# Weight conversion beside the first feed-forward block: a fixed order of instructions in place of a generator, and earlier maxima in attention

## Chip, cores, metric

One core of one Trainium2 chip. The metric is the device time of one execution in microseconds; several executions of a kernel are timed and their median is given.

## What is computed

Attention over 32 heads (4 batches of 8 heads, 576 positions, 64 channels; block mask of 64 positions), then two feed-forward stages on the 2304 x 512 result:

```python
scores = where(block_i >= block_j, q @ k.T / 8, -1e9)
x = softmax(scores) @ v                                # 2304 x 512
h = x @ w_in;  x = (h * cos(h)) @ w_out                # 512 -> 2048 -> 512
P = exp(x @ w_gate - max), 8 times normalised over rows and columns
out = sum over 8 experts e of P[:, e] * (relu(x @ w1[e]) @ w2[e])
```

`w_in` and `w_out` arrive as 64-bit floats and are turned into 32-bit floats on the core ("conversion"). Each 32-bit operand of a large product is split into a high and a low part, and three products (high x high, high x low, low x high) are added in PSUM.

## The kernel before

The order on each engine is written by hand: an engine executes its instructions in the order in which the code issues them.

**Attention.** A loop runs over 32 heads. For each, PE forms trial scores (`px`, L290), DVE takes their maxima (L312) into `nm`, PE transposes them (`turn`, L317, tile `pt`), DVE writes them into the query tile (`maxima`, L321), PE computes scores (L329, then L330, which reads that query tile), ACT takes exponentials and PE multiplies with V in five pieces (`pv`, L357). Head i+1's maxima are prepared during head i: `turn` stands between pieces 3 and 4 of `pv`.

**Conversion.** The weights of the first feed-forward stage come in 32 halves of 128 x 512 numbers, each a load of 512 KB (L91). Converting one half takes two ACT instructions (L103, L109), three on DVE (L114, L118, L125) and one on POOL (L131). A generator yields these as five steps; `some` and `convert` take a number of steps from it. Eight halves are converted during attention (one in four heads), the other 24 in the first block of the feed-forward stage, two a unit. Two tiles hold loads, one tile the magnitudes (`sc`).

**First feed-forward stage.** `moe1` runs 48 units: 3 blocks of 768 tokens, in each 16 units of 128 hidden features. Unit n computes on PE the products a and b of `hidden` (two tiles `h` of 384 columns, 12 matmuls each) and then, for unit n-1, `o_part` (24 matmuls, L760, into six accumulators `acc`). Between them each product passes `reduce_h` (DVE L725 to an integer `ki`, L727 to `r`), `sine` (ACT L732), `times` (DVE L736 to `g`), `g_hi` (ACT L740 to `hh`) and `g_lo` (DVE L744 to `hl`). `wsplit` splits a converted half for PE: `jh` on ACT (L66), `jl` on POOL (L69). The weights of unit 0's hidden product are split at the end of attention into a free corner of `xh` and `xl` (`spare`).

**Queues.** SP issues all DMAs in order. An issue waits at the queue's head until the tile that it writes is free.

The rest (two more blocks, then the experts, from about 645 us on) is not changed.

Of the kernel before, what the change touches and what calls it, by code (L numbers as in the profile page):

```python
# [22 lines left out]
NC = DM // 128  # L23
# [20 lines left out]
def attention_moe_kernel(ctx: ExitStack, tc: tile.TileContext, qk, v, w_a, gate, w_b, out):  # L44
# [26 lines left out]
    raw = [None] * F1  # L71
    spare = [x[:, NC - 1, (B - 1) * S:(B - 1) * S + DM] for x in (xh, xl)]

# [4 lines left out]
    class Conv:  # L78
        def __init__(self, w64, sc):
            self.w64, self.sc, self.own = {}, {}, (w64, sc)  # L80

        def scratch(self, i, k, shape):
            n = int(np.prod(shape[1:]))
            flat = self.own[i][:, k % 2 * n:(k % 2 + 1) * n]
            return flat if len(shape) == 2 else flat.rearrange("p (n w) -> p n w", w=shape[2])

        def load(self, i):
            k = ORDER[i]
            self.w64[i] = self.scratch(0, i, [128, DM, 2])
            src = w_a[k // 2].bitcast(I32).rearrange("p (n w) -> p n w", w=2)  # L90
            nc.sync.dma_start(out=self.w64[i], in_=src[:, (k % 2) * DM:(k % 2 + 1) * DM, :])  # L91

# [6 lines left out]

        def magnitude(self, k):  # L100

            self.sc[k] = self.own[1]
            nc.scalar.activation(self.sc[k].bitcast(F32), self.high(k).bitcast(F32), AF.Abs)  # L103

        def rounding(self, k):
# [3 lines left out]
            nc.scalar.activation(w64[:, :, 0], mid, AF.Copy, scale=2.0 ** -13)  # L109

# [17 lines left out]
        def add(self, k):  # L128

            m = self.part(k).bitcast(I32)  # L130
            nc.gpsimd.tensor_tensor(out=m, in0=m, in1=self.w64.pop(k)[:, :, 0], op=ALU.add)  # L131

# [19 lines left out]
    def attention():  # L152
        with tc.tile_pool(name="at1", bufs=1) as p1, tc.tile_pool(name="at2", bufs=2) as p2, \
# [290 lines left out]
            for i in range(NH):  # L444
# [62 lines left out]
            n = F1 + 1  # L507
            return conv, conv_gen, {0: lambda: spread(e - 2), n: lambda: (x_hi(e - 4), x_lo(e - 4)), n + 1: lambda: scale(e - 2),
                              n + 2: lambda: (x_hi(e - 2), fetch(e)),
                              n + 3: lambda: (x_lo(e - 2), invert(e), give(e)), n + 4: lambda: spread(e),  # L510
                              n + 6: lambda: scale(e), n + 7: lambda: x_hi(e), n + 8: lambda: x_lo(e)}

    with tc.manual_schedule():
        conv, conv_gen, leftover = attention()
        psh = ctx.enter_context(tc.tile_pool(name="psh", bufs=2, space=PSUM))

# [4 lines left out]

        def hidden(wh, wl, t0):
            ps = psh.tile([128, TB], F32, tag="h", name="h")
# [181 lines left out]
        def moe1():  # L705
            nonlocal th, tl
            with tc.tile_pool(name="m1", bufs=2) as p:
# [6 lines left out]

                def wsplit(n, part, lo_eng=nc.gpsimd):
                    if 0 <= n < NU:
                        hi = p.tile([128, DM], F32R, tag=f"jh{part}", name="jh")
                        lo = p.tile([128, DM], F32R, tag=f"jl{part}", name="jl")
                        split(hi, lo, raw[units[n][1]][:, part * DM:(part + 1) * DM], nc.scalar, lo_eng)
                        wj[n, part] = (hi, lo)  # L720

                def reduce_h(ps):
                    ki = p.tile([128, TB], I32, tag="ki", name="ki", bufs=1)
                    r = p.tile([128, TB], F32, tag="r", name="r")
                    nc.vector.tensor_scalar(out=ki, in0=ps, scalar1=float(1 / TWO_PI), scalar2=0.25,  # L725
                                            op0=ALU.mult, op1=ALU.add)
# [47 lines left out]

                wj[0, 0] = spare
                last = NU - F1

                todo = iter(range(NH // 4 + 1, NHALF))

                def convert(n):  # L780
                    for _ in range(n):
                        next(conv_gen, None)
                    k = next(todo, None)
                    if k is not None:
                        conv.load(k)

# [12 lines left out]
                tgen = None  # L799
                convert(1)  # L800
                for n in range(NU + 1):
                    if n == F1 + 10:
                        th = post.tile([128, 3, 2, TB], F32R, tag="th", name="th", bufs=1)
                        tl = post.tile([128, 3, 2, TB], F32R, tag="tl", name="tl", bufs=1)
                        tgen = tprep(0, nc.vector)
                    if n < NU:
                        t0 = units[n][0] * HB
                        w = wj.pop((n, 0))
                        G[n] = (p.tile([128, HB], F32R, tag="hh", name="hh"),
                                p.tile([128, HB], F32R, tag="hl", name="hl"))  # L810
# [7 lines left out]
                        sine(ra)  # L818
                        if n:
                            wsplit(n + 1, 0)  # L820
                        ga = times(pa, ra)
# [239 lines left out]
```

## Time and profile before

| | us |
|---|---|
| median of 3 executions | 2176.4 (2174.54 to 2180.85) |
| the profiled execution, its time | 2170.81 |
| its span | 2169.0 |
| attention, up to the first `hidden` | 0 to 198.95 |
| first block, units 0 to 12 | 198.95 to 337.46 |
| first block, units 13 to 15 | 337.46 to 362.60 |

Busy shares of the span: PE 98%, DVE 68%, ACT 45%, POOL 41%. A row of the timeline gives start, duration, engine, source line, operation, output and inputs by the program's names, and in brackets how long the engine had been idle and what ended it. Where several like instructions follow each other they stand in one row (x2). PE's matmuls overlap; their distance from start to start says more than their durations.

### The profile page before, as it was taken

To read this page: it belongs to the slowest core of one execution; us is meant where nothing else is said; L and a number is where in the kernel's file an instruction comes from. 1 tells how busy PE (TensorE), PEld (TensorE's weight loads), DVE (VectorE), ACT (ScalarE), POOL (GpSimd) and SP (SyncE) were. 2 spreads that over 40 slices of the span, in tenths; PEclk is the share of its full clock that TensorE was granted. 3 is DMA by queue.
4 is the path that set the end of the run, shared out by engine and by line. 5 is a ranking of instruction groups with operands and counts; after the bars stand their busy time and mean duration, and the time that the engine had idled before them with its cause. 6 is when DMAs were issued, how large, how long until landed. Compare 5 with 4: busy or idle time off the path is not lost.

```text
span 2169.0 us, 29774 instructions
## 1 busy us (share of the span) xinstructions
PE 2130.2 (98%) x10959; PEld 1894.2 (87%) x10959; DVE 1474.4 (68%) x2426; ACT 968.4 (45%) x1814; POOL 899.9 (41%) x815
## 2 busy tenths in 40 slices
PE   9999889999999999999999999999999999999999
PEld 7787779998998888888898888889898888889898
DVE  7776666566667866666766666666767666666665
ACT  7886554434444333433434333433434333433432
POOL 4453443333323434434563434434563434434341
PEclk9999999999999999999999999999999999999999
DMA  6674330001001212212122211212122212212120
GB/s 166 173 182 120 101 98 1 7 1 40 1 21 59 73 64 66 71 59 78 59 78 88 74 62 63 74 59 78 59 79 88 72 65 64 73 59 78 59 78 29
DMA packets 74161, 152.84 MB, mean 70 GB/s; under 512 B 32896, under 2 KB 32896, under 8 KB 74016
## 3 DMA queue, kind: packets, MB, share of 16 engines
q1 hardware_dynamic: 74016, 150.95, 22.4%
q8 instruction: 86, 1.41, 0.3%
q14 instruction: 59, 0.48, 0.1%
HBM read 136.91 MB, written 4.87 MB: 65 GB/s over the span
## 4 chain that ended last, share of the span: by engine, by line
PE 81%; DVE 6%; issue 5%; POOL 3%; DMA 2%; ACT 2%; SPq 0%; POOLq 0%; ACTq 0%; DVEq 0%
PE acc L518 12%; PE acc L520 12%; PE acc L519 12%; PE hx L520 6%; PE hx L518 6%; PE hx L519 6%; PE acc L760 4%; PE o L357 3%; PE hy L520 3%; PE hy L518 3%; PE hy L519 3%; POOL jl L69 2%; DMA cw<-in_w_a_dram 2%; PE hz L518 1%; PE hz L520 1%
## 5 line engine op out<-in xcount | busy, mean ns | idle before, releaser
L628 POOL TENSOR_TENSOR wv<-stg,wv 128x512 fp32r<-128x512 f32 x190 | 333.7, 1778 | 853.5 <-ACT wv L627 853.5
L518 PE MATMUL acc<-wv,hh 128*128 128x512 f32 x1152 | 456.7, 396 | 0.0
L520 PE MATMUL acc<-wv,hl 128*128 128x512 f32 x1152 | 455.5, 395 | 0.0
L519 PE MATMUL acc<-wv,hh 128*128 128x512 f32 x1152 | 454.5, 395 | 0.0
L945 DVE SCALAR_TENSOR_TENSOR oa<-acc,P,oa 128x512 f32<-128x512 f32 x540 | 379.1, 740 | 4.9 <-PE acc L520 4.3
L916 ACT ACTIVATE hh<-c 128x384 fp32r<-128x384 f32 x288 | 151.3, 525 | 407.5 <-DVE c L1001 167.2
L917 DVE SCALAR_TENSOR_TENSOR hl<-c,hh 128x384 fp32r<-128x384 f32 x288 | 164.0, 569 | 176.4 <-ACT hh L916 176.4
L520 PEld LDWEIGHTS acc<-wv,hl 128*128 128x128 f32 x1152 | 216.0, 187 | 53.7
L519 PEld LDWEIGHTS acc<-wv,hh 128*128 128x128 f32 x1152 | 215.9, 187 | 43.9
L518 PEld LDWEIGHTS acc<-wv,hh 128*128 128x128 f32 x1152 | 216.1, 188 | 42.9
L69 POOL TENSOR_TENSOR jl<-raw,jh 128x512 fp32r<-128x512 f32 x95 | 131.8, 1393 | 220.1 <-ACT jh L66 214.7
L994 DVE TENSOR_TENSOR c<-hz,c 128x384 f32<-128x384 f32 x96 | 53.4, 557 | 190.8 <-PE hz L520 190.8
L619 DVE TENSOR_TENSOR wal<-s,wah 128x1024 fp32r<-128x1024 f32 x96 | 171.4, 1786 | 0.0
L984 ACT ACTIVATE c<-hx 128x384 f32<-128x384 f32 x95 | 46.9, 494 | 275.0 <-PE hx L520 275.0
L520 PE MATMUL hy<-xh,wal 128*128 128x384 f32 x384 | 128.8, 335 | 1.0 <-DVE wal L619 1.0
L518 PE MATMUL hx<-th,wah 128*128 128x384 f32 x384 | 128.7, 335 | 0.7 <-ACT c L984 0.7
L518 PE MATMUL h<-xh,jh 128*128 128x384 f32 x376 | 126.7, 337 | 2.4 <-DVE g L736 2.4
L518 PE MATMUL hy<-xh,wah 128*128 128x384 f32 x384 | 128.6, 335 | 0.4 <-DVE c L1001 0.2
L520 PE MATMUL hx<-th,wal 128*128 128x384 f32 x384 | 128.5, 335 | 0.0
L519 PE MATMUL hy<-xl,wah 128*128 128x384 f32 x384 | 128.3, 334 | 0.0
L519 PE MATMUL hx<-tl,wah 128*128 128x384 f32 x384 | 128.3, 334 | 0.0
L520 PE MATMUL h<-xh,jl 128*128 128x384 f32 x376 | 126.5, 337 | 1.6 <-POOL jl L69 1.6
(223 smaller groups left out, 4779.7 us busy)
## 6 DMA issues: line engine op xcount, KB each, us to landing
stg<-in_w_b_dram SPq DMA_DIRECT2D x192, 512.0 KB
cw<-in_w_a_dram SPq DMA_DIRECT2D x32, 512.0 KB
st<-in_qk_dram SPq DMA_DIRECT2D x64, 144.0 KB
v<-in_v_dram SPq DMA_DIRECT2D x31, 160.0 KB
tt<-inv SPq DMA_DIRECT2D x32, 144.0 KB
out_dram<-oa SPq DMA_DIRECT2D x18, 256.0 KB
kb<-qb SPq DMA_DIRECT2D x31, 144.0 KB
qb<-qa SPq DMA_DIRECT2D x31, 144.0 KB
```

The source lines that it names most:

```text
L69: eng_lo.tensor_tensor(out=lo, in0=src, in1=hi.bitcast(F32), op=ALU.subtract)
L357: nc.tensor.matmul(o[:, q0:q1], vt[:, c], e, start=c == 0, stop=True, skip_group_check=c > 0)
L518: nc.tensor.matmul(ps, lh, rh, start=first, stop=False, skip_group_check=go_on)
L519: nc.tensor.matmul(ps, lh, rl, start=False, stop=False, skip_group_check=go_on)
L520: nc.tensor.matmul(ps, ll, rh, start=False, stop=last, skip_group_check=go_on)
L619: eng.tensor_tensor(out=self.al, in0=self.s, in1=self.ah.bitcast(F32), op=ALU.subtract)
L628: eng.tensor_tensor(out=t[:, DM:2 * DM], in0=src, in1=t[:, 0:DM].bitcast(F32), op=ALU.subtract)
L760: nc.tensor.matmul(acc[half, b][:, at:at + w_], w[:, s], h[:, t0:t0 + w_], start=f == 0 and i == 0 and at == 0, stop=f == F1 - 1 and i == ...
L916: nc.scalar.activation(hh, src, AF.Relu)
L917: nc.vector.scalar_tensor_tensor(out=hl, in0=src, scalar=0.0, in1=hh.bitcast(F32), op0=ALU.max, op1=ALU.subtract)
L945: nc.vector.scalar_tensor_tensor(out=o, in0=acc, scalar=p, in1=o, op0=ALU.mult, op1=ALU.add)
L994: nc.vector.tensor_tensor(out=c[0], in0=z, in1=c[0], op=ALU.add)
```

## The change

In attention the transposition and `maxima` of the next head stand ahead of piece 3 of `pv` instead of behind it. Loads of words to convert are cut in quarters of 128 KB, one in each head from head 4 on. The last three heads split three halves into corners of `xh` and `xl` (for unit 0, both, and unit 1's hidden weights).

In the first block a function `unit` takes the place of generator and `wsplit`. 14 units convert 2, 2, 2, 1, 2, 2, 1, 2, 2, 2, 1, 2, 2, 1 halves. There are three tiles for loads (the third is `w3`) and two pairs for magnitudes and rounding words; a half's load is issued three halves ahead, and its POOL addition is made in the following unit. The first step of `reduce_h` goes from DVE to ACT, `jl` of the next hidden weights from POOL to DVE. Unit 1 puts its two products into the banks of the accumulators a11 and a12.

```diff
                 pv(i, 1)
                 pv(i, 2)
-                pv(i, 3)
                 if nxt:
                     turn(i + 1)
                     maxima(i + 1)
+                pv(i, 3)
                 pv(i, 4)
...
-                if i % 4 == 0 and i:
-                    conv.load(i // 4 + 1)
+                if i >= 4:
+                    conv.load(i // 4 + 1, None, i % 4)
...
-                if i == NH - 1:
-                    split(*spare, raw[0][:, 0:DM], nc.scalar, nc.gpsimd)
+                if i >= NH - 3:
+                    j = i - (NH - 3)
+                    f, o = FIRST[j][0], FIRST[j][1] * DM
+                    split(*SPARE[j], raw[f][:, o:o + DM], nc.scalar, nc.gpsimd)
...
+                    if by_act:
+                        nc.scalar.activation(ki, ps, AF.Identity, bias=quarter, scale=float(1 / TWO_PI))
...
+                def fetch(k):
+                    if k < NHALF:
+                        j = (k - FIRST_HALF) % 3
+                        conv.load(k, w3 if j == 2 else conv.own[0][:, j * 2 * DM:(j + 1) * 2 * DM])
+
+                def unit(n):
+                    t0 = units[n][0] * HB
+                    w = wj.pop((n, 0))
+                    ks = [todo.pop(0) for _ in range(share[n])] if n < FRAMES else []
+                    own = [pbank.tile([128, 512], F32, tag=t, name="h")[:, 0:TB] if n == 1 else None
+                           for t in ("a11", "a12")]
+                    pa = hidden(*w, t0, own[0])
+                    ra = reduce_h(pa, True)
+                    if (n, 1) not in wj:
+                        w_hi(n, 1)
+                        w_lo(n, 1)
+                    for k in adds:
+                        conv.add(k)
+                    adds[:] = ks
+                    sine(ra)
+                    pb = hidden(*w, t0 + TB, own[1])
+                    new = (n + 1, 0) not in wj
+                    if new:
+                        w_hi(n + 1, 0)
+                    ga = times(pa, ra)
+                    if new:
+                        w_lo(n + 1, 0, nc.vector)
+                    rb = reduce_h(pb, True)
+                    g_hi(n, 0, ga)
+                    g_lo(n, 0, ga)
+                    sine(rb)
+                    for k in ks[0:1]:
+                        conv.magnitude(k, more[k % 2][0])
+                    gb = times(pb, rb)
+                    g_hi(n, 1, gb)
+                    g_lo(n, 1, gb)
+                    for k in ks[1:2]:
+                        conv.magnitude(k, more[k % 2][0])
+                    for k in ks:
+                        conv.rounding(k, more[k % 2][1])
+                    for k in ks:
+                        conv.clamp(k)
+                        conv.shift(k)
+                        conv.bits(k)
+                        fetch(k + 3)
...
-                        if n == 0:
-                            wsplit(1, 0)
-                        elif units[n - 1][1]:
+                    if n < F1:
+                        unit(n)
+                    elif n < NU:
...
-                        convert(5)
                         gb = times(pb, rb)
                         g_hi(n, 1, gb)
                         g_lo(n, 1, gb)
                         if units[n][1] == 0:
                             wsplit(n, 1)
-                        convert(5)
```

On DVE a unit of the first block stood like this before (`ki`, `r`, `g` and `hl` are the steps named above, `tla` and `raw` the conversion):

```order
L725 TENSOR_SCALAR ki<-h 128x384
L727 SCALAR_TENSOR_TENSOR r<-ki,h 128x384
L736 TENSOR_TENSOR g<-h,r 128x384
L725 TENSOR_SCALAR ki<-h 128x384
L727 SCALAR_TENSOR_TENSOR r<-ki,h 128x384
L744 TENSOR_TENSOR hl<-g,hh 128x384
L114 TENSOR_SCALAR tla<-tla 128x512
L118 TENSOR_SCALAR tla<-tla 128x512
L125 SCALAR_TENSOR_TENSOR raw<-cw,tla 128x512
L736 TENSOR_TENSOR g<-h,r 128x384
L744 TENSOR_TENSOR hl<-g,hh 128x384
```

and now, in a unit with two halves (`tt` is the second magnitude tile):

```order
L744 SCALAR_TENSOR_TENSOR r<-ki,h 128x384
L753 TENSOR_TENSOR g<-h,r 128x384
L728 TENSOR_TENSOR jl<-raw,jh 128x512
L744 SCALAR_TENSOR_TENSOR r<-ki,h 128x384
L761 TENSOR_TENSOR hl<-g,hh 128x384
L753 TENSOR_TENSOR g<-h,r 128x384
L761 TENSOR_TENSOR hl<-g,hh 128x384
L114 TENSOR_SCALAR tla<-tla 128x512
L118 TENSOR_SCALAR tla<-tla 128x512
L125 SCALAR_TENSOR_TENSOR raw<-cw,tla 128x512
L114 TENSOR_SCALAR tt<-tt 128x512
L118 TENSOR_SCALAR tt<-tt 128x512
```

The `ki` rows are gone, `jl` has come, and both conversions stand behind the second `hl` instead of one between the halves of the unit and one at its end.

On ACT a unit stood like this (`jh` is the high part of the weights, `tla<-cw` the magnitude, which reads the load):

```order
L66 ACTIVATE jh<-raw 128x512
L732 ACTIVATE r<-r,half_pi 128x384
L66 ACTIVATE jh<-raw 128x512
L740 ACTIVATE hh<-g 128x384
L732 ACTIVATE r<-r,half_pi 128x384
L109 ACTIVATE cw<-cw 128x512
L103 ACTIVATE tla<-cw 128x512
L740 ACTIVATE hh<-g 128x384
L109 ACTIVATE cw<-cw 128x512
L103 ACTIVATE tla<-cw 128x512
```

and now:

```order
L740 ACTIVATE ki<-h,quarter 128x384
L723 ACTIVATE jh<-raw 128x512
L749 ACTIVATE r<-r,half_pi 128x384
L723 ACTIVATE jh<-raw 128x512
L740 ACTIVATE ki<-h,quarter 128x384
L757 ACTIVATE hh<-g 128x384
L749 ACTIVATE r<-r,half_pi 128x384
L102 ACTIVATE tla<-cw 128x512
L757 ACTIVATE hh<-g 128x384
L102 ACTIVATE tt<-w_2383 128x512
L109 ACTIVATE rawl<-cw 128x512
L109 ACTIVATE tla<-w_2383 128x512
```

The magnitude that stood last in a unit, right ahead of the next unit's `jh`, now stands ahead of the second `hh` or behind it, and the unit ends with the two roundings. `w_2383` is the third load tile.

On PE in attention the transposition `pt` stood behind the `ep` piece (128x192 or 65x192, piece 3):

```order
L290 MATMUL px<-ka,qa_99 128x320
L357 MATMUL o<-er,v_108 65x128
L357 MATMUL o<-er,v_108 65x320
L357 MATMUL o<-ec,v_108 65x320
L357 MATMUL o<-ep,v_108 65x192
L317 MATMUL pt<-ident,nm_106 101x128
L357 MATMUL o<-eq,v_108 65x64
```

and now stands ahead of it:

```order
L291 MATMUL px<-ka,qa_100 128x320
L358 MATMUL o<-er,v_109 65x128
L358 MATMUL o<-er,v_109 65x320
L358 MATMUL o<-ec,v_109 65x320
L318 MATMUL pt<-ident,nm_107 101x128
L358 MATMUL o<-ep,v_109 65x192
L358 MATMUL o<-eq,v_109 65x64
```

Only the transposition has moved, by one piece; the maxima on DVE ahead of it keep their place.

## Rows read from the trace of the kernel before

**Rows 1.** Stretches of the first feed-forward block, one each: its units 3 to 12, 13 to 15.

```profile
core 0: us, PE busy (x) PEld busy (x) DVE busy (x) ACT busy (x) POOL busy (x), PEclk, DMA share, GB/s
230.23:337.46 107.23, 92.03 (x482) 80.53 (x480) 75.76 (x140) 54.46 (x98) 50.72 (x41) 0.97 0.28 89
337.46:362.60 25.14, 25.14 (x146) 23.55 (x144) 14.64 (x27) 9.99 (x18) 7.50 (x7) 1.00 0.00 1
```

**Rows 2.** Chain that ended last, units 5 and 6: start us, us, what.

```profile
252.45 3.53 DMA cw<-in_w_a_dram
...
263.33 3.52 DMA cw<-in_w_a_dram
```

**Rows 3.** Timeline of PE: start us, us, instruction, idle before and releaser.

```profile
198.95 0.42 PE L518 MATMUL h<-xh 128*128 128x384 f32 x1
...
200.26 0.44 PE L520 MATMUL h<-xh,xl 128*128 128x384 f32 x1 [0.72 <-POOL xl L69]
...
224.41 1.01 PE L760 MATMUL acc<-hh,jh 128*128 128x512 f32 x2 [3.60 <-ACT jh L66]
...
230.23 0.34 PE L518 MATMUL h<-xh,jh 128*128 128x384 f32 x1
...
337.46 0.34 PE L518 MATMUL h<-xh,jh 128*128 128x384 f32 x1
```

**Rows 4.** Timeline of DVE in unit 14, which converts nothing.

```profile
348.74 0.55 DVE L727 SCALAR_TENSOR_TENSOR r<-ki,h 128x384 f32<-128x384 int32 x1
...
350.04 0.56 DVE L736 TENSOR_TENSOR g<-h,r 128x384 f32<-128x384 f32 x1 [0.74 <-ACT r L732]
...
352.40 0.56 DVE L736 TENSOR_TENSOR g<-h,r 128x384 f32<-128x384 f32 x1
...
353.55 0.56 DVE L744 TENSOR_TENSOR hl<-g,hh 128x384 fp32r<-128x384 f32 x1 [0.59 <-ACT hh L740]
```

**Rows 5.** Timeline of DVE: one conversion's first instruction, and the one behind it.

```profile
329.52 0.41 DVE L114 TENSOR_SCALAR tla<-tla 128x512 f32<-128x512 f32 x1
...
331.04 0.55 DVE L725 TENSOR_SCALAR ki<-h 128x384 int32<-128x384 f32 x1
```

**Rows 6.** ACT reading a product from PSUM (all, by lines): busy us, mean ns.

```profile
L984 ACT ACTIVATE c<-hx 128x384 f32<-128x384 f32 x95 | 46.9, 494 | 275.0 <-PE hx L520 275.0
```

**Rows 7.** Timeline of ACT in unit 0.

```profile
201.73 1.28 ACT L732 ACT_TABLE_LOAD   x1
```

**Rows 8.** Timelines of DVE and POOL in units 1 and 5.

```profile
209.53 1.32 POOL L69 TENSOR_TENSOR jl<-raw,jh 128x512 fp32r<-128x512 f32 x1 [0.26 <-ACT jh L66]
...
209.62 1.52 DVE L114 TENSOR_SCALAR tla<-tla 128x512 f32<-128x512 f32 x1
...
259.32 1.01 DVE L744 TENSOR_TENSOR hl<-g,hh 128x384 fp32r<-128x384 f32 x1
```

**Rows 9.** Timelines of DVE and PE in attention, one head to the next.

```profile
85.57 1.02 DVE L312 TENSOR_REDUCE nm<-px 128x1 f32<-128x448 f32 x2 [0.65 <-PE px L290]
...
86.67 0.49 PE L357 MATMUL o<-ep,v 128*65 128x192 f32 x2
86.99 0.27 PE L317 MATMUL pt<-ident,nm 128*101 128x128 f32 x1
...
87.78 0.28 PE L329 MATMUL sp<-qb,kb 128*128 128x256 f32 x1
88.19 0.39 PE L330 MATMUL sp<-qa,ka 101*128 101x256 f32 x1
88.41 0.31 PE L329 MATMUL sp<-qb,kb 128*128 128x320 f32 x1
88.56 0.31 PE L330 MATMUL sp<-qa,ka 101*128 101x320 f32 x1
```

**Rows 10.** Timeline of PE where a head waits for a move.

```profile
70.54 0.36 PE L329 MATMUL sp<-qb,kb 128*128 128x256 f32 x1 [1.18 <-issue]
```

**Rows 11.** Stretch of PE behind the idle time in unit 2.

```profile
224.40:226.00 1.60, 1.59 (x5) 1.28 (x6) 1.08 (x3) 1.44 (x3) 1.57 (x2) 0.50 0.76 264
```

More of the change, by code (lines that the diff above doesn't have):

```diff
@@ L52, in attention_moe_kernel @@
     nc.vector.memset(ones, 1.0)
+    quarter = top.tile([128, 1], F32, name="quarter")
     half_pi = top.tile([128, 1], F32, name="half_pi")
@@ L71, in attention_moe_kernel @@
     raw = [None] * F1
-    spare = [x[:, NC - 1, (B - 1) * S:(B - 1) * S + DM] for x in (xh, xl)]
+    SPARE = [[x[:, NC - 1 - j, (B - 1) * S:(B - 1) * S + DM] for x in (xh, xl)] for j in range(3)]
+    FIRST = ((0, 0), (1, 0), (0, 1))
     NHALF = 2 * F1
@@ L79, in __init__, with load @@
         def __init__(self, w64, sc):
[L80 to L87, printed above, removed]
-            k = ORDER[i]
-            self.w64[i] = self.scratch(0, i, [128, DM, 2])
-            src = w_a[k // 2].bitcast(I32).rearrange("p (n w) -> p n w", w=2)
-            nc.sync.dma_start(out=self.w64[i], in_=src[:, (k % 2) * DM:(k % 2 + 1) * DM, :])
+            self.w64, self.sc, self.cw, self.own = {}, {}, {}, (w64, sc)
+        def load(self, i, flat=None, quarter=None):
+            k = ORDER[i]
+            flat = self.own[0][:, i % 2 * 2 * DM:(i % 2 + 1) * 2 * DM] if flat is None else flat
+            self.w64[i] = flat.rearrange("p (n w) -> p n w", w=2)
+            src = w_a[k // 2].bitcast(I32).rearrange("p (n w) -> p n w", w=2)[:, (k % 2) * DM:(k % 2 + 1) * DM, :]
+            s = slice(0, DM) if quarter is None else slice(quarter * DM // 4, (quarter + 1) * DM // 4)
+            nc.sync.dma_start(out=self.w64[i][:, s, :], in_=src[:, s, :])
         def high(self, i):
@@ L98, in part, with magnitude, rounding @@
             return raw[f][:, o:o + DM]
-        def magnitude(self, k):
-            self.sc[k] = self.own[1]
+        def magnitude(self, k, sc=None):
+            self.sc[k] = self.own[1] if sc is None else sc
             nc.scalar.activation(self.sc[k].bitcast(F32), self.high(k).bitcast(F32), AF.Abs)
-        def rounding(self, k):
+        def rounding(self, k, out=None):
             w64 = self.w64[k]
             mid = w64.rearrange("p n w -> p (n w)").bitcast(U16).rearrange("p (n q) -> p n q", q=4)[:, :, 1]
-            nc.scalar.activation(w64[:, :, 0], mid, AF.Copy, scale=2.0 ** -13)
+            self.cw[k] = w64[:, :, 0] if out is None else out
+            nc.scalar.activation(self.cw[k], mid, AF.Copy, scale=2.0 ** -13)
         def clamp(self, k):
@@ L130, in add @@
             m = self.part(k).bitcast(I32)
-            nc.gpsimd.tensor_tensor(out=m, in0=m, in1=self.w64.pop(k)[:, :, 0], op=ALU.add)
+            nc.gpsimd.tensor_tensor(out=m, in0=m, in1=self.cw.pop(k), op=ALU.add)
         def run(self):
@@ L507, in attention @@
             n = F1 + 1
-            return conv, conv_gen, {0: lambda: spread(e - 2), n: lambda: (x_hi(e - 4), x_lo(e - 4)), n + 1: lambda: scale(e - 2),
+            more = [(tla[:, 0:DM], odd_sums[0][:, 0:DM]), (tt[0][:, 0:DM], RAW[1][:, 0:DM])]
+            return conv, [[t.bitcast(I32) for t in pair] for pair in more], {0: lambda: spread(e - 2), n: lambda: (x_hi(e - 4), x_lo(e - 4)), n + 1: lambda: scale(e - 2),
                               n + 2: lambda: (x_hi(e - 2), fetch(e)),
@@ L513, in attention_moe_kernel @@
     with tc.manual_schedule():
-        conv, conv_gen, leftover = attention()
+        conv, more, leftover = attention()
         psh = ctx.enter_context(tc.tile_pool(name="psh", bufs=2, space=PSUM))
@@ L520, in mm3, with hidden @@
             nc.tensor.matmul(ps, ll, rh, start=False, stop=last, skip_group_check=go_on)
-        def hidden(wh, wl, t0):
-            ps = psh.tile([128, TB], F32, tag="h", name="h")
+        def hidden(wh, wl, t0, ps=None):
+            if ps is None:
+                ps = psh.tile([128, TB], F32, tag="h", name="h")
             for c in range(NC):
@@ L713, in moe1, with w_hi, w_lo, wsplit @@
                 PLACE = [[(0, 0, 0, 512), (1, 0, 512, 256)], [(1, 256, 0, 256), (2, 0, 256, 512)]]
[L715 to L722, printed above, removed]
+                def w_hi(n, part):
+                    hi = p.tile([128, DM], F32R, tag=f"jh{part}", name="jh")
+                    lo = p.tile([128, DM], F32R, tag=f"jl{part}", name="jl")
+                    nc.scalar.activation(hi, raw[units[n][1]][:, part * DM:(part + 1) * DM], AF.Copy)
+                    wj[n, part] = (hi, lo)
+                def w_lo(n, part, eng=nc.gpsimd):
+                    hi, lo = wj[n, part]
+                    eng.tensor_tensor(out=lo, in0=raw[units[n][1]][:, part * DM:(part + 1) * DM],
+                                      in1=hi.bitcast(F32), op=ALU.subtract)
+                def wsplit(n, part):
+                    if 0 <= n < NU and (n, part) not in wj:
+                        w_hi(n, part)
+                        w_lo(n, part)
+                def reduce_h(ps, by_act=False):
                     ki = p.tile([128, TB], I32, tag="ki", name="ki", bufs=1)
                     r = p.tile([128, TB], F32, tag="r", name="r")
-                    nc.vector.tensor_scalar(out=ki, in0=ps, scalar1=float(1 / TWO_PI), scalar2=0.25,
-                                            op0=ALU.mult, op1=ALU.add)
+                    if by_act:
+                        nc.scalar.activation(ki, ps, AF.Identity, bias=quarter, scale=float(1 / TWO_PI))
+                    else:
+                        nc.vector.tensor_scalar(out=ki, in0=ps, scalar1=float(1 / TWO_PI), scalar2=0.25,
+                                                op0=ALU.mult, op1=ALU.add)
                     nc.vector.scalar_tensor_tensor(out=r, in0=ki, scalar=float(-TWO_PI), in1=ps,
@@ L773, in evacuate @@
                                                         in1=xh[:, c, cols].bitcast(F32), op=ALU.subtract)
-                wj[0, 0] = spare
+                for j, unit in enumerate(FIRST):
+                    wj[unit] = SPARE[j]
                 last = NU - F1
[L778 to L785, printed above, removed]
+                FIRST_HALF, FRAMES = NH // 4, 14
@@ new lines, in moe1 @@
+                w3 = p.tile([128, 4 * HK], F32, tag="s", name="w3", bufs=1).bitcast(I32)
+                todo = list(range(FIRST_HALF, NHALF))
+                share = [((n + 1) * len(todo) + FRAMES - 1) // FRAMES - (n * len(todo) + FRAMES - 1) // FRAMES
+                         for n in range(FRAMES)]
+                adds = []
+                def fetch(k):
+                    if k < NHALF:
+                        j = (k - FIRST_HALF) % 3
+                        conv.load(k, w3 if j == 2 else conv.own[0][:, j * 2 * DM:(j + 1) * 2 * DM])
@@ L799, in moe1 @@
                 tgen = None
-                convert(1)
+                fetch(FIRST_HALF + 1)
+                fetch(FIRST_HALF + 2)
                 for n in range(NU + 1):
@@ L806, in moe1 @@
                     if n < NU:
+                        G[n] = (p.tile([128, HB], F32R, tag="hh", name="hh"),
+                                p.tile([128, HB], F32R, tag="hl", name="hl"))
+                    if n < F1:
+                        unit(n)
+                    elif n < NU:
                         t0 = units[n][0] * HB
                         w = wj.pop((n, 0))
[L809 to L813 removed]
+                        if units[n - 1][1]:
                             wsplit(n - 1, 1)
```

4 lines of the change are left out of this document (2 added, 2 removed).

## The prediction

> **What bounds the kernel now.** I read the busy shares first (PE 98%), then the stretches, to see where the missing 2% lie. From unit 13 on, PE is busy all the time: three units take 25.14 us, 8.38 each. The ten units before them take 107.23, 10.72 each, with PE busy 92.03 of it [rows 1]. The same matmuls therefore cost 2.34 us more a unit where weights are converted. The chain of waits says why: once a unit it runs through a load of words to convert, 3.5 us long, at a distance of 10.9 us [rows 2]. The load waits for its tile, ACT's magnitude waits for the load, and behind it in ACT's order stands `jh`, which PE wants. It is a ring of waits: DVE is busy 7.6 us a unit there and ACT 5.4 [rows 1], both under 8.38. Attention is nearly a PE stage; what it loses a head is taken from single rows below.
>
> **First block, from unit 2 on.** Work moves off the ring: loads go out three halves ahead, about one and a half units, against 3.5 us for one [rows 2]; so the load leaves the chain. The halves are also early enough: unit m splits at most the half in place 2m+2 of the order of conversion, and the closest case is unit 9, which wants place 20 and has 21 after unit 8's additions. What is late next is DVE, in its new order. From `r` of product a to its `g` it takes 1.30 us, as ACT's sine lies between; from the second `g` to the second `hl` 1.15, for `hh`; the last `hl` 0.56 [rows 4]. One conversion takes 1.52 [rows 5]. `jl` on DVE with 512 columns is not in the rows; scaled from `hl` it is 0.56 x 512/384 = 0.75, at best `hl`'s 0.56, at worst 2.0, the 0.75 behind one whole POOL instruction. I take 0.75.
> The step: `r` 0, `g` 1.30, `jl` 1.88, second `r` 2.63, second `g` 3.93, second `hl` 5.08, two conversions from 5.66 to 8.70. A unit with one half ends at 7.18. Units 2 to 13 hold eight of the first and four of the second: 8 x 8.70 + 4 x 7.18 = 98.3, against 12 x 8.38 = 100.6 on PE. So DVE just keeps up, if nothing disturbs it.
> POOL does. It has one `jl` and up to two additions a unit, each about 1.32, now beside DVE's `jl` and first `hl`. In the trace a clamp that takes 0.41 [rows 5] took 1.52, to about the end of the POOL instruction beside it, and an `hl` of 0.56 took 1.01 [rows 8]. If each such meeting blocks, `jl` waits from 1.88 to the end of POOL's second instruction (2.6), the third holds back `hl` to 4.5, and the second `g` goes to 5.0: a unit takes 9.8, with one addition 9.3, with one half 8.2. Five, three and four of these are 109.7: 9.1 over PE. A unit's `jl` is done 3.2 to 3.9 after product a's end (`r` starts 0.6 after it) and wanted 8.38 - 2.1 + 0.3 = 6.6 after it, so 2.7 to 3.4 are to spare, of which about 1 is used up when unit 2 starts, so 7 would reach PE. Between 0 and 7 I take 3.5.
> By the Trainium skill, "SBUF — State Buffer", section "Who interferes with whom", VectorE and GpSimd share a port pair as an exclusive lock: with two SBUF inputs or in a two-port mode the later one stands still for the earlier one's whole instruction. The clamp's 1.52 us agrees. By that rule alone the block loses the 7, by the undisturbed rows nothing; the first is rival 1.
>
> **First block, start.** Counted from the first `hidden` matmul (198.95 [rows 3]; PE's 24 `hidden` and 24 `o_part` matmuls have equally many columns, so 2.1 us for each product or half of `o_part`). The 0.72 that PE waits for POOL's split [rows 3] goes, as it is made two heads earlier. Product a ends at 2.1. `ki` moves to ACT, at 0.49 for reading PSUM [rows 6], at worst 0.62, about the same as on DVE. Then ACT loads a table, 1.28 [rows 7], then sine: `g` at 2.1 + 2.55. Through the steps above unit 0's second `hl` ends at 8.3 and its two conversions at 11.3; only there may unit 1's `r` begin. Its `g` ends at 13.2, its second `g` at 15.8. PE, however, is through with unit 1's products at 8.4 and half of `o_part` at 10.5; the other half writes into a11 and a12, which hold those products until these two `g` are done. PE stands still for about 2.7 and then 1.7 us, and unit 2 starts at 16.9. POOL beside it costs 0 to 1.2 (0.6). Behind 3.60 us without work PE's clock stood at half [rows 11], 1.2 GHz, and 4.2 us of work took 5.8 (224.41 to 230.23 [rows 3]); here 0 to 1.6 (0.8). Unit 2 starts at 18.3.
> Sum: 18.3 + 11 x 8.38 + 3.5 = 114.0 to unit 13's start, which now lies at 337.46 - 198.95 = 138.5. Gain 24.5. From there on both run at PE's pace.
>
> **Attention.** From the first score product to the third 0.63 us pass, where 0.15 a 320-column product [rows 9] makes 0.12 + 0.12: 0.39 is lost for the query tile with the maxima. The transposition starts at 86.99; ahead of piece 3 it could start at 86.67, but the reductions end at 86.59, and PE must be told and load them as weights: between 86.67 and 86.99, I take 86.81. The chain from it through `maxima` to the scores comes 0.18 earlier; PE itself waits 0.14 ahead of it, which the 0.39 covers. 30 heads x 0.18 = 5.4. At best 30 x 0.32 = 9.6; at worst the transposition waits and nothing comes back, 30 x 0.14 = 4.2 lost.
> Loads in quarters: SP issues some 20 more, ahead of the next head's move of the high part of q. I cost this at nothing, hidden by the head that lies between this move and its use. Without that cover it is 1.18 on PE, seen once [rows 10]; at best that one goes, at worst each of the 7 old load times has one, 8 us. I take 0, as one in 31 is what the rows show. Two more splits on ACT and POOL in the last heads stand where heads 32 and up would have been prepared.
>
> **Sum.** 24.5 + 5.4 = 30 us, on the profiled execution 2170.8 to 2141. The median before is 5.6 above that execution; I keep the distance: 2146.
>
> **Rivals.**
> 1. *The lock holds at each meeting.* For it the 1.52 row, against it that 0.56 grew to only 1.01 [rows 8]. Unit 2 at 16.9 + 1.2 + 1.6 = 19.7, then 92.2 + 7: 118.9, gain 19.6 + 5.4: 2151.
> 2. *Clean.* DVE keeps up and the clock holds: 16.9 + 92.2 = 109.1, gain 29.4, attention 30 x 0.3 = 9: 2138. For it the 98.3; against it POOL's 3.9 us a unit.
> 3. *Attention gives nothing or lengthens,* as the transposition waits for the reductions (0.08 us between them and its new place): 24.5 - 4.2 = 20.3: 2156.
> 4. *Slower: DVE and POOL take turns.* If DVE loses all of POOL's time in each unit (3.9, 2.6 with one addition), units take 12.6, 11.3 and 11.1: 5 x 12.6 + 3 x 11.3 + 4 x 11.1 = 141.3, 38.9 of it on PE after the slack; unit 2 at 16.9 + 3.9 + 1.6 = 22.4, unit 13 at 153.5, a loss of 15.0 less 5.4: 2186. It decides from about 11 us a DVE round. Against it: POOL was as busy before, 5.1 us a unit [rows 1], with DVE's sum at 7.6.
> 5. *The loads stay on the chain,* units at 10.7 as now; only attention gains: 2171. Against it the three tiles.
>
> **Numbers.** Forecast 40%, rivals 25, 15, 12, 4, 4%. A change under 0.3% (6.5 us) cannot be told from none. Forecast and rivals 1 to 3 are faster by more, 92%; rival 5 within, 4%; rival 4 slower, 4%. The range runs from rival 2's 2138 less 2 to rival 3's 2156 plus 4, for the load's unknown: 2136 to 2160, which leaves out both last rivals and some of the tails.
>
> **What would show it.** Units 3 to 12 8.4 to 8.9 apart on PE and no load in the chain of waits; a DVE round between 8.7 and 9.8 with `jl` drawn out beside POOL; two gaps of some 2 us on PE in the first `o_part`, ended by `g`; heads 0.1 to 0.3 shorter, with PE waiting for the reductions ahead of the transposition. Wrong it is if units stay above 10 us, if `o_part` does not wait for a11 and a12, or if heads get no shorter.

## The result, and the profile after

The changed kernel takes 2144.79 us (median of four runs, 2142.92 to 2146.37), the kernel before beside it 2175.47. The ratio is 0.9857, its 95% interval 0.9834 to 0.9879: faster, 1.2 us under the forecast. The profiled execution spans 2141.1 us, 27.9 less than before.

Stretches of the changed kernel: units 0 and 1, unit 2, units 3 to 12, units 13 to 15, 3.2 us of unit 14 from 316.40 on (columns as in [rows 1]).

```profile
core 0: us, PE busy (x) PEld busy (x) DVE busy (x) ACT busy (x) POOL busy (x), PEclk, DMA share, GB/s
189.38:208.40 19.02, 14.87 (x76) 13.45 (x74) 12.13 (x21) 14.26 (x25) 5.45 (x5) 0.87 0.42 127
208.40:217.65 9.25, 9.25 (x49) 8.72 (x48) 6.29 (x12) 5.53 (x11) 4.61 (x3) 0.90 0.40 115
217.65:304.29 86.64, 84.83 (x481) 78.42 (x480) 71.68 (x118) 58.95 (x111) 38.62 (x27) 1.00 0.32 101
304.29:334.67 30.38, 27.08 (x145) 24.78 (x144) 22.84 (x39) 17.42 (x33) 8.14 (x7) 0.94 0.03 9
316.40:319.60 3.20, 3.20 (x10) 3.06 (x11) 2.40 (x5) 2.75 (x6) 0.00 (x0) 0.51 0.00 0
```

Timeline of PE, the rows that answer to [rows 3]: first `hidden` matmul, the two gaps in unit 0's output product, unit 14.

```profile
189.38 0.42 PE L522 MATMUL h<-xh 128*128 128x384 f32 x1
...
203.62 0.58 PE L777 MATMUL acc<-hh,xh 128*128 128x256 f32 x1 [3.32 <-DVE g L753]
...
206.53 0.80 PE L777 MATMUL acc<-hh,xh 128*128 128x512 f32 x1 [0.83 <-DVE g L753]
...
316.40 0.66 PE L522 MATMUL h<-xh,jh 128*128 128x384 f32 x1 [3.13 <-DVE g L753]
```

So the 27.9 us are three terms. Attention is 198.95 - 189.38 = 9.57 shorter. From the first `hidden` matmul to unit 13 it takes 304.29 - 189.38 = 114.91 instead of 138.51: 23.60 gained. Units 13 to 15 take 30.38 instead of 25.14 [rows 1]: 5.24 lost.

A round is the time from one unit's first `r` on DVE to the next unit's. One with two halves, units 8 to 9 (timeline of DVE; cut to the ends and what is drawn out; the last conversion's `raw<-cw,tt` comes right behind the last row of the order given for DVE above):

```profile
264.92 0.54 DVE L744 SCALAR_TENSOR_TENSOR r<-ki,h 128x384 f32<-128x384 int32 x1
266.14 0.56 DVE L753 TENSOR_TENSOR g<-h,r 128x384 f32<-128x384 f32 x1 [0.68 <-ACT r L749]
266.72 1.23 DVE L728 TENSOR_TENSOR jl<-raw,jh 128x512 fp32r<-128x512 f32 x1
...
271.65 0.69 DVE L125 SCALAR_TENSOR_TENSOR raw<-w,tla 128x512 int32<-128x512 int32 x1
...
273.18 1.71 DVE L125 SCALAR_TENSOR_TENSOR raw<-cw,tt 128x512 int32<-128x512 int32 x1
274.81 0.54 DVE L744 SCALAR_TENSOR_TENSOR r<-ki,h 128x384 f32<-128x384 int32 x1
```

POOL beside it:

```profile
266.12 1.29 POOL L131 TENSOR_TENSOR raw<-raw,tla 128x512 int32<-128x512 int32 x1
273.05 1.30 POOL L728 TENSOR_TENSOR jl<-raw,jh 128x512 fp32r<-128x512 f32 x1 [5.64 <-ACT jh L723]
274.30 1.75 POOL L131 TENSOR_TENSOR raw<-raw,rawl 128x512 int32<-128x512 int32 x1
```

The round is 9.89 us long. It is one of the long ones: rounds with two halves take 8.6 to 8.7 in units 2 and 4, 9.6 in unit 5 and 9.9 to 10.0 from unit 7 to 11; those with one half take 8.14, 7.67 and 7.32 (units 3, 6, 10). The last conversion starts 0.13 behind POOL's `jl` and takes 1.71 where its twin takes 0.69; `jl` on DVE takes 1.23 beside an addition. `g`, which reads PSUM and one tile, keeps 0.56 beside the same addition. POOL's addition at 274.30 in turn takes 1.75, as the conversion is still going. These rows agree with the exclusive lock in the Trainium skill, "SBUF — State Buffer", section "Who interferes with whom".

DVE ahead of unit 13's `r` (the gate's weights are split here, at n = 12):

```profile
311.77 1.27 DVE L69 CAST ghl<-g 128x32 fp32r<-128x32 f32 x1
313.07 1.20 DVE L70 TENSOR_TENSOR ghl<-g,ghl 128x32 fp32r<-128x32 f32 x1
...
314.47 0.55 DVE L744 SCALAR_TENSOR_TENSOR r<-ki,h 128x384 f32<-128x384 int32 x1
```

A step that the prediction never looked at stands 2.7 us long in DVE's order, just where DVE is latest: `r` begins 10.18 us after PE began unit 13. PE waits 3.13 us for `g`, then runs 3.2 us at 0.51 of its clock. In the kernel before the same step took 1.7 us, its second instruction already beside a POOL instruction (337.09, 1.29 us):

```profile
337.21 1.22 DVE L69 TENSOR_TENSOR ghl<-g,ghl 128x32 fp32r<-128x32 f32 x1
```

There it cost nothing: DVE then waited 1.05 us for PE's product, its `r` (340.36) began 2.90 us after PE began unit 13, and PE was busy all the time [rows 1].

In attention the rows that answer to [rows 9] are these (PE):

```profile
82.64 0.34 PE L318 MATMUL pt<-ident,nm 128*101 128x128 f32 x1
82.81 0.49 PE L358 MATMUL o<-ep,v 128*65 128x192 f32 x2
...
83.81 0.28 PE L330 MATMUL sp<-qb,kb 128*128 128x256 f32 x1
83.93 0.35 PE L331 MATMUL sp<-qa,ka 101*128 101x256 f32 x1
84.12 0.32 PE L330 MATMUL sp<-qb,kb 128*128 128x320 f32 x1
```

First to third score product take 0.31 us instead of 0.63, and heads follow each other at 5.61 instead of 5.86. PE does not wait ahead of the transposition: it starts 0.08 after DVE's reductions end (82.56). The single stalls of before, such as [rows 10], are gone too.

### The profile page after: what moved, and what is told of

Its sections match the earlier page's. It is cut to its first block, busy times and chain, and to the rows that moved or that the text cites. A ratio compares the mean times of both kernels' runs of the same rounds, so it can differ in the third digit from the quotient of the medians.

```text
span 2141.1 us, 29753 instructions
## 1 busy us (share of the span) xinstructions
PE 2120.3 (99%) x10959; PEld 1892.6 (88%) x10959; DVE 1476.5 (69%) x2409; ACT 979.1 (46%) x1846; POOL 885.4 (41%) x801
## 4 chain that ended last, share of the span: by engine, by line
PE 84%; DVE 7%; issue 5%; POOL 2%; ACT 2%; DMA 0%; POOLq 0%; ACTq 0%; DVEq 0%
PE acc L522 12%; PE acc L524 12%; PE acc L523 12%; PE hx L524 6%; PE hx L522 6%; PE hx L523 6%; PE o L358 4%; PE acc L777 3%; PE hy L524 3%; PE hy L522 3%; PE hy L523 3%; POOL jl L728 2%; PE hz L524 2%; PE hz L523 2%; PE hz L522 2%
## 5 line engine op out<-in xcount | busy, mean ns | idle before, releaser
L728 POOL TENSOR_TENSOR jl<-raw,jh 128x512 fp32r<-128x512 f32 x78 | 111.1, 1425 | 270.8 <-ACT jh L723 260.5
L749 ACT ACTIVATE r<-r,half_pi 128x384 f32<-128x384 f32 x96 | 59.3, 617 | 162.5 <-DVE r L744 162.2
```

Of the source, the lines that this page charges most:

```text
L728: eng.tensor_tensor(out=lo, in0=raw[units[n][1]][:, part * DM:(part + 1) * DM], in1=hi.bitcast(F32), op=ALU.subtract)
L749: nc.scalar.activation(r, r, AF.Sin, bias=half_pi)
```

## Experiments

Medians; each ratio is against runs of the kernel before on the same chip. The medians of the kernel before lie between 2172.80 and 2175.47 in these series, so differences of 2 to 3 us between two experiments are read from the traces. "H" is the first `hidden` matmul of the profiled execution: 198.95 before, 189.38 changed.

**1. The gate's split at unit 20.**

```
-  steps[12 - last] = [gate_prep]
+  steps[20 - last] = [gate_prep]
```

> The changed kernel with one edit: the gate's weights are split at unit 20 instead of unit 12 (they are first used at unit 25). In the changed kernel DVE does this split at 311.77 to 314.47, ahead of unit 13's r, while it is behind PE, and units 13 to 15 take 30.38 us (304.29 to 334.67) where three take 25.14 undisturbed. Theory A (queue and clock): without these 2.7 us in DVE's way PE waits about 0.4 instead of 3.13 us in unit 14, and so its clock does not fall to half behind the wait (about 1.7 us); units 13 to 15 take 25.5 to 26, the time falls by 4.5 to 2140. Theory B (only the queue counts, the clock falls all the same): 2.7 less, 2142. Theory C (DVE is late by itself at the end of the conversions, the split only stands beside it): unit 13 to 15 stay near 30, 2145, or the split costs the same at its new place.

2140.38 us, ratio 0.9851 (0.9836 to 0.9866). The interval overlaps that of the changed kernel; the trace decides. Units 13 to 15:

```profile
305.20:332.29 27.09, 25.93 (x145) 23.45 (x144) 20.52 (x35) 17.31 (x33) 8.53 (x7) 1.00 0.03 10
```

3.3 us less, 2.1 of it waits and 1.2 busy time of PE, whose clock stays full: theory A, short by 1.2, since PE still waits 1.15 us there for a DVE that is late from before (`r` of unit 13 begins 7.52 after PE began the unit). At its new place the split takes 1.7 us (375.02) and PE doesn't wait, as DVE has time there. (Unit 2 took 1.0 us longer in this execution, the clock staying at half for longer behind the same two gaps.)

**2. No own banks for unit 1.**

```
-  if n == 1 else None
+  if n == -1 else None
```

> The changed kernel with unit 1's two products in the two buffers that all other units use, instead of in two accumulators' banks (a11, a12), for whose release PE waits 3.32 and 0.83 us in the first half of unit 0's output product. Theory A (DVE sets the block): DVE is busy from unit 1's r (201.78) to unit 13's without a gap except 1.58 us ahead of unit 2's r; so unit 2 starts some 4 to 5 us earlier, about 13.7 to 14.5 us after the first hidden matmul instead of 19.0, but by unit 13 only the 1.6 us of that gap are left of it: 2143, and PE's waits come back in the units between. Theory B (the start is a delay of its own, as the prediction's sum has it): unit 13 too is 4 to 5 us earlier, 2140. Theory C: with two buffers the first units wait for each other and nothing is gained, 2145 or more.

2143.19 us, ratio 0.9866 (0.9852 to 0.9879). Units 0 and 1, units 2 to 12, units 13 to 15, part of unit 14:

```profile
190.45:204.80 14.35, 13.08 (x75) 11.99 (x74) 8.31 (x15) 10.53 (x18) 4.97 (x5) 1.00 0.41 120
204.80:305.56 100.76, 95.62 (x528) 85.87 (x529) 82.70 (x135) 67.53 (x128) 43.29 (x31) 1.00 0.32 104
305.56:336.44 30.88, 27.47 (x146) 24.98 (x145) 22.66 (x39) 17.38 (x33) 8.50 (x7) 0.94 0.03 9
319.50:322.70 3.20, 3.20 (x12) 3.20 (x12) 2.54 (x6) 2.61 (x5) 0.46 (x1) 0.50 0.00 0
```

Unit 2 starts 14.35 after H instead of 19.02, and unit 13 at 115.11 instead of 114.91. Theory A, to the point that not even 1.6 us are left: DVE sets the pace of the block from unit 1's `r` on, and what PE doesn't wait at the start it waits later, in pieces of 0.19 to 0.57 us.

**3. POOL's work left out.** The additions are not made, and the low part of the second weight halves is zeros written by ACT.

```
-  conv.add(k)
+  conv.cw.pop(k)
-  w_lo(n, 1)
+  nc.scalar.activation(wj[n, 1][1], raw[units[n][1]][:, DM:2 * DM], AF.Copy, scale=0.0)
```

> The changed kernel with nearly all POOL work of the converting units left out: the additions of the rounding words are not made, and the low part of the second weight halves is written as zeros by ACT instead of by POOL's subtraction (0.6 us more on ACT a unit). Theory lock: the second bits instruction falls from 1.7 to 0.69 us and jl on DVE from 1.23 to 0.69, a DVE round with two halves from 9.88 to about 8.7, one with a single half stays near 7.2; PE's waits for DVE between units 8 and 14 (0.27 to 0.56, and 3.13) vanish, unit 13 starts 111 to 112 after the first hidden matmul instead of 114.9, units 13 to 15 take under 26.5 with the gate's split where it is, the time is 2136. Rival: DVE's rounds are that long by DVE's and ACT's own order: they stay at 9.9, 2145.

2134.92 us, ratio 0.9823 (0.9808 to 0.9838). Units 3 to 12 and 13 to 15, then DVE:

```profile
215.73:299.53 83.80, 83.80 (x482) 78.51 (x480) 62.40 (x122) 66.09 (x125) 0.00 (x0) 1.00 0.33 108
299.53:324.67 25.14, 25.14 (x146) 23.55 (x144) 16.27 (x35) 16.59 (x32) 0.00 (x0) 1.00 0.00 1
```

```profile
269.47 0.55 DVE L744 SCALAR_TENSOR_TENSOR r<-ki,h 128x384 f32<-128x384 int32 x1
...
271.22 0.69 DVE L728 TENSOR_TENSOR jl<-raw,jh 128x512 fp32r<-128x512 f32 x1
...
277.13 0.69 DVE L125 SCALAR_TENSOR_TENSOR raw<-w,tt 128x512 int32<-128x512 int32 x1
277.74 0.55 DVE L744 SCALAR_TENSOR_TENSOR r<-ki,h 128x384 f32<-128x384 int32 x1
...
302.72 0.17 DVE L69 CAST ghl<-g 128x32 fp32r<-128x32 f32 x1
```

The lock: the same instructions fall to 0.69 us, the gate's two to 0.17 and 0.19 at their old place, the round to 8.27, and PE is busy throughout.

**4. `jl` of the next unit on POOL again.**

```
-  w_lo(n + 1, 0, nc.vector)
+  w_lo(n + 1, 0)
```

> The changed kernel with one part undone: the low half jl of the next unit's first weights is made by POOL again, not by DVE. POOL then has four instructions of 1.3 us a two-half unit in a row, and jl is the last of them. Theory lock: DVE is spared 1.23 us and loses as much to more meetings (hl beside POOL), rounds of 9.3 to 10.3, and jl comes some 1 us later to PE: 2145 to 2150. Rival: DVE's round falls to 8.7, PE keeps its pace: 2138.

2140.04 us, ratio 0.9846 (0.9832 to 0.9859; overlapping the changed kernel's). DVE with the next `hl`, one of the meetings, and units 13 to 15:

```profile
282.86 0.55 DVE L744 SCALAR_TENSOR_TENSOR r<-ki,h 128x384 f32<-128x384 int32 x1
...
285.55 1.53 DVE L761 TENSOR_TENSOR hl<-g,hh 128x384 fp32r<-128x384 f32 x1
```

```profile
304.81:330.76 25.95, 25.45 (x145) 23.41 (x144) 18.44 (x31) 14.79 (x28) 12.46 (x10) 1.00 0.00 1
```

Both theories miss. Rounds of 9.9 fell only to 9.3 (273.60 to 282.86) with new meetings, as the lock theory had it, and PE now waits 0.5 us for `jl` at times; unit 13 comes no earlier (115.4 after H). But DVE is less late there (`r` begins 5.59 after PE began the unit), the gate's split takes 1.7 instead of 2.7, and units 13 to 15 take 4.4 less. With the gate's split at unit 12, `jl` on DVE brought the changed kernel nothing.

**5. POOL's work placed beside PSUM reads and waits** (gate's split at unit 20; the edit is shortened, its conditions are left out).

```
 ra = reduce_h(pa, True)
-w_hi(n, 1); w_lo(n, 1)
-for k in adds:
+for k in reversed(adds):
     conv.add(k)
 sine(ra)
 pb = hidden(*w, t0 + TB, own[1])
-w_hi(n + 1, 0)
 ga = times(pa, ra)
-w_lo(n + 1, 0, nc.vector)
 rb = reduce_h(pb, True)
+w_hi(n + 1, 0); w_lo(n + 1, 0, nc.vector)
 g_hi(n, 0, ga)
 g_lo(n, 0, ga)
 sine(rb)
+w_hi(n, 1); w_lo(n, 1)
```

> The changed kernel with the gate's split at unit 20 and another order in the converting units, made so that POOL works while DVE reads PSUM or waits: POOL adds the unit's later half first (it is ready just as r begins) and makes jl of the unit's second weights last; ACT makes their high half behind the second sine; DVE takes the second r ahead of the next unit's jl. By hand from the rows of the changed kernel: r 0, g 1.2, second r 1.75, jl 2.6 (behind POOL's second addition), hl 3.25, second g 3.8, second hl 5.25, conversions 5.75 to 8.65. Theory lock: a round takes 8.65 instead of 9.88, PE keeps its pace, unit 13 starts 111 to 112 after the first hidden matmul, units 13 to 15 take 25.2 to 25.6: 2135. Rival: the meetings only move, the rounds stay at 9.5 to 9.9: 2140, as with the gate's split moved alone. Third: the late jl makes the output products wait: over 2141.

2133.89 us, ratio 0.9818 (0.9805 to 0.9831). POOL, then DVE in one round, then units 3 to 12 and 13 to 15:

```profile
270.30 1.30 POOL L131 TENSOR_TENSOR raw<-raw,tla 128x512 int32<-128x512 int32 x1 [3.61 <-DVE raw L125]
271.55 1.31 POOL L131 TENSOR_TENSOR raw<-raw,rawl 128x512 int32<-128x512 int32 x1
273.83 1.29 POOL L728 TENSOR_TENSOR jl<-raw,jh 128x512 fp32r<-128x512 f32 x1 [0.97 <-POOL raw L131]
```

```profile
270.07 0.55 DVE L744 SCALAR_TENSOR_TENSOR r<-ki,h 128x384 f32<-128x384 int32 x1
...
272.35 1.06 DVE L728 TENSOR_TENSOR jl<-raw,jh 128x512 fp32r<-128x512 f32 x1
...
277.90 0.69 DVE L125 SCALAR_TENSOR_TENSOR raw<-w,tt 128x512 int32<-128x512 int32 x1
278.51 0.55 DVE L744 SCALAR_TENSOR_TENSOR r<-ki,h 128x384 f32<-128x384 int32 x1
```

```profile
216.31:300.11 83.80, 83.80 (x481) 78.53 (x480) 65.91 (x122) 60.38 (x115) 34.84 (x27) 1.00 0.33 108
300.11:325.25 25.14, 25.14 (x145) 23.57 (x144) 17.08 (x31) 15.38 (x29) 7.85 (x7) 1.00 0.00 1
```

With all work done the round is 8.44 us, and PE is never idle from unit 2 on, as where POOL's work was left out. One meeting is left: `jl` on DVE takes 1.06 beside POOL's second addition. Against experiment 1, which has the gate's split at the same place, this is 6.5 us less by the medians.

**6. The same without own banks** (edit of experiment 2).

> The kernel with the other order and the gate's split at unit 20, and unit 1's products in the two common buffers instead of a11 and a12. Where DVE set the block, these banks made no difference (unit 13 came 115.1 instead of 114.9 after the first hidden matmul). Theory: with rounds of 8.43 and 7.2 DVE needs (8 x 8.43 + 4 x 7.2) / 12 = 8.0 a unit, less than PE's 8.38, so now the start is a delay of its own: unit 2 starts 14.4 instead of 17.6 after the first hidden matmul and without the half clock behind it (0.7), and unit 13 comes 3.9 earlier: 2130. Rival: DVE, behind since unit 1, is still late at unit 13, the gain is under 1: 2133 to 2134.

2129.58 us, ratio 0.9796 (0.9782 to 0.9809): the best version, 15.2 under the changed kernel by the medians, some 13 by the ratios. Units 0 and 1, then 2 to 12:

```profile
189.46:203.60 14.14, 12.91 (x76) 12.06 (x74) 8.11 (x16) 10.80 (x19) 3.74 (x4) 1.00 0.45 131
203.60:296.20 92.60, 92.45 (x530) 86.21 (x528) 74.47 (x138) 68.99 (x131) 40.05 (x32) 1.00 0.36 115
```

Unit 13 comes 106.74 after H (110.47 in experiment 5): the edit that gave nothing while DVE set the pace gives 3.7 once PE does.

**7. The maxima behind product 3 again.**

```
 pv(i, 2)
+pv(i, 3)
 if nxt:
     turn(i + 1)
     maxima(i + 1)
-pv(i, 3)
```

> The changed kernel with the transposition and the maxima put back behind V product 3; the quarter loads, the earlier splits and the first block stay as changed. Theory M: the move alone gives the shorter heads, 5.61 instead of 5.86 us: heads go back to 5.86, the first hidden matmul from 189.38 to about 197 (30 x 0.25), the time to 2152. By the prediction's 0.18 a head: 194.8 and 2150. Rival: what shortened attention is the quarter loads and the absence of the stall of 1.18 and its like: the first hidden matmul stays within 1 us of 189.4 and the time near 2145.

2151.75 us, ratio 0.9904 (0.989 to 0.9917), H at 197.04, heads 5.85 apart, without single stalls: theory M.

**8. Whole loads again.**

```
-if i >= 4:
-    conv.load(i // 4 + 1, None, i % 4)
+if i % 4 == 0 and i:
+    conv.load(i // 4 + 1)
```

> The changed kernel with a whole half of the words to convert loaded every fourth head, as before, instead of a quarter a head; all else as changed. Theory: of the 9.57 us that attention gained, 7.5 are the moved maxima and some 2 the single stalls of before (1.18 at 70.54 and others), which came from whole loads that hold up the move of the next head's query part: the stalls come back, the first hidden matmul is at about 191.4 instead of 189.38, the time is 2147. Rival: the loads do not matter, as the prediction priced them: first hidden matmul within 0.5 of 189.4, 2145. Third: whole loads collide worse with the shorter heads: over 3 us lost.

2156.99 us, ratio 0.9924 (0.9912 to 0.9937), H at 200.61 in an execution of 2153.13: 11 us lost in attention, the third case. PE in an early head with a load, then PE and ACT in the worst head (9.06 us from one transposition to the next):

```profile
45.31 0.36 PE L330 MATMUL sp<-qb,kb 128*128 128x256 f32 x1 [0.51 <-DMA qb<-qa]
...
93.55 0.36 PE L330 MATMUL sp<-qb,kb 128*128 128x256 f32 x1 [1.66 <-issue]
```

```profile
93.49 0.65 ACT L367 ACTIVATE tla<-o 64x576 f32<-64x576 f32 x1 [2.79 <-DMA sums<-tla]
```

PE's row at 93.55 names no cause. The same instruction at 45.31 waits for the move of q (`qb<-qa`), which SP issues right behind the 512 KB, and in experiment 10, where the load is issued behind that move, PE shows no wait at this instruction; so the move is the likely cause, though this row doesn't say it. ACT waits at the same time for another transfer: the evacuation of the odd head overwrites the row of sums of the even one, and that row's small transfer has not left, for SP issued 512 KB ahead of it. At the stall of before [rows 10] ACT waits for it too, 1.81 us up to 70.04.

Not all of the loss is waiting. Behind its 1.66 us the worst head ran at a granted clock of 0.51 from 94.20 to 97.40, which makes about 1.6 of the 3.45 us that it takes over 5.61. The other runs with whole loads and early maxima (experiments 9 to 11) also have such a stretch behind their longest stall; attention in the kernel before, in the changed one and in experiment 7 has none.

**9. Only the maxima, in the kernel before** (the edit of experiment 7 reversed, nothing else of the change).

> The kernel before with one part of the change alone: the transposition and the maxima ahead of V product 3. Whole loads every fourth head stay, and the first block is the old one. Theory (a pair): the move pays only together with the quarter loads, since with whole loads and the moved maxima the heads that carry a load became 0.4 to 3.5 us longer than 5.6; the first hidden matmul comes at 200 to 201 (198.95 before), the time is 2172 to 2176, no gain. Rival (the parts add up): heads of 5.61, 30 x 0.25 = 7.5 gained, first hidden matmul at 191.5, time 2165.

2172.64 us, ratio 0.9996 (0.9987 to 1.0004), H at 201.34: the parts don't add up. Undisturbed heads are 5.6 us apart as in the changed kernel, the loss lies in heads with a load (up to 8.05). Of attention's two edits the maxima alone lose 2.4 us of H, the quarters without them (experiment 7, which has the earlier splits too) gain 1.9, both together 9.57.

**10 and 11. Whole loads, issued later:** behind the next head's move of q, or further back, behind the even head's row of sums as well. Both leave the quarter loads out.

```
 if nxt:
     move_q_hi(i + 1)
+if i % 4 == 1 and i > 1:        # 10
+    conv.load(i // 4 + 1)
 ...
 sums(i - 1)
+if i % 4 == 1 and i > 1:        # 11, instead
+    conv.load(i // 4 + 1)
 ...
-if i >= 4:
-    conv.load(i // 4 + 1, None, i % 4)
```

> The changed kernel with whole loads every fourth head, but issued behind the next head's move of the high part of q (one head later in the order) instead of ahead of it. Theory queue: in the whole-load run the move waited behind 512 KB, up to 3.5 us; behind the move the load finds cover until the next head's, the first hidden matmul comes at 189.4 to 191.5 (200.6 with whole loads ahead of the move), the time is 2145 to 2147. Rival (size): 512 KB at a time hold up other transfers of a head all the same (V, the low part of k, the next q and k): 195 or later, 2150 and more.

> As the run with whole loads behind the move of q, but issued one place later still: behind V's load and behind the transfer of the even head's row of sums (2.2 KB). In both runs with whole loads, and in the kernel before at its stall of 1.18 us, ACT's evacuation of the odd head waited 1.8 to 3.3 us for that small transfer, which stood behind the 512 KB. Theory sums: with the row of sums ahead of the load these waits go, the first hidden matmul comes at 189.4 to 192 (201.73 with the load ahead of the sums), the time is 2145 to 2147, and quarters are not needed. Rival (size): what the load holds up is then the next transfer, the low part of k or the next q and k: 195 or later, 2150 and more.

Run 10: 2157.31 us, ratio 0.9921 (0.9907 to 0.9935), H at 201.73. Run 11: 2152.07, 0.9902 (0.9885 to 0.9918), H at 201.52. The rival both times. ACT in run 10, DVE and PE in run 11:

```profile
118.32 0.65 ACT L367 ACTIVATE tla<-o 64x576 f32<-64x576 f32 x1 [3.33 <-DMA sums<-tla]
```

```profile
173.34 0.25 DVE L379 RECIPROCAL sc<-sc 72x16 f32<-72x16 f32 x1 [1.92 <-DMA sc<-sums]
```

```profile
176.06 0.53 PE L318 MATMUL pt<-ident,nm 128*101 128x128 f32 x1 [2.46 <-DVE nm L313]
```

In run 10 ACT's wait reaches PE through the exponentials `ep` (2.33 us at 120.26). In run 11, with the row of sums ahead of the load, ACT's wait for it falls to 1.04 at most, and DVE waits for the fetch of the sums instead, in front of its reductions, 1.46 to 1.94 us, some 12 us behind each load from the one at 87.95 on. How the load brings that about isn't shown: the one ahead of 173.34 was issued at 160.89, and the DMA share between 166 and 167 was 0.08. Whole loads cost 11 us of H or more at each of three places, and quarters at the first of them cost none: that speaks for the size and not the place.

## Why the prediction held, and where it did not

- *The loads leave the chain; the halves are early enough:* right. No load is in the chain of waits of the changed block. No run takes the third tile, the earlier issue or the move of `ki` to ACT back alone, so how the 23.60 us divide between them is not shown.
- *Start, unit 2 at 18.3 after H:* 19.02, with the two gaps where they were said to be (2.7 and 1.7 forecast, 3.32 and 0.83 seen) and half clock behind the first, up to about 210.4 in unit 2. But it is not a term of the sum. Experiment 2 takes 4.7 us of it away and unit 13 comes no earlier. That 114.0 to unit 13 came so near to 114.91 is luck in part: DVE's order from unit 1 on sets this time, not PE's start with DVE's loss added.
- *DVE and POOL, 3.5 between 0 and 7:* from unit 2 to 13 the loss is 114.91 - 19.02 - 92.2 = 3.7, of which 0.87 is unit 2 at the half clock, which the prediction had counted in its start; 2.8 lie in units 3 to 12. The upper bound's two-half round of 9.8 is what the later rounds take (9.89), but with other meetings: from unit 7 on the last of two conversions, not `hl`, is blocked by POOL's `jl`. The one-half rounds of 8.2 are 8.14, 7.67 and 7.32, and POOL is blocked as well, which the working had left out. Experiments 3 and 5 show the lock from both sides.
- *"From there on both run at PE's pace":* this step failed, by 5.24 us. The prediction asked what the change moves, not what else stands in DVE's order while DVE is late. The gate's split took 1.7 us before, where DVE had time for it, and takes 2.7 now, where it has none; experiment 1 brings 3.3 back. The other 1.9 is DVE's own lateness, which the working compared with PE's pace only up to unit 13. Experiments 3 and 5 bring back all of it.
- *Attention, 30 x 0.18 = 5.4:* mis-sized; measured 9.57. The transposition doesn't wait the 0.14 us that the working gave it, so the scores come 0.32 closer together and not 0.18; a head gains 0.25, or 7.5 in all, and some 2 are single stalls. *"I cost this at nothing"* of the quarter loads was the other half of the error: without them the moved maxima gain nothing (experiment 9). A kernel with that part alone has rival 3's outcome, though not its reason: what lengthens it are the heads with a load.

So 4.2 us more in attention and 5.2 less in units 13 to 15 nearly cancel; that the total of 2146 is nearer than its terms is luck. What stays open is the size of the pair: why heads of 5.61 us lose 11 us to whole loads and heads of 5.86 only 2. That small transfers wait is shown, and that PE's clock falls to half behind the longest stall (some 1.6 us of the 11); how much slack a head had for the waits is not shown.

## What to carry to other kernels

Where two engines are nearly level, a wait at the start and a wait later are one and the same; add them up only after finding the engine whose own chain sets the pace, and look at everything in its order, also at what the change does not touch. Place POOL's work beside VectorE's PSUM reads and its waits for ScalarE: that was worth as much here as leaving POOL's work out. Price a large transfer by what stands behind it in the queue, small transfers too: a row of 2.2 KB waited up to 3.33 us here. Where PE shows a wait for nothing, look at like instructions that do name a cause, and at what ScalarE waits for at the same time, which need not be the same thing.

## What the hardware showed beside

- An instruction of 0.17 us (128x32) took 1.27 beside POOL: the price of a meeting does not follow the size of the instruction that waits.
- In experiment 2 PE waited 3.15 us up to 317.74; its matmuls then ran at full pace until 319.4 and at half from 319.5 to 322.7 (granted clock 0.50). In the changed kernel, after 3.13 us, they ran at half at once, from 316.40 to 319.60 (0.51).
- Behind the same two gaps (3.32 and 0.83) unit 2 took 9.25 in the changed kernel and 10.26 in experiment 1, at a granted clock of 0.90 and 0.80.
